# Loading half a weight matrix in three transfers instead of two, and splitting each transpose copy between VectorE and ScalarE

## Chip, cores and metric

The kernel runs on one core of one Trainium2 chip (trn2). The metric is the time of one launch on the device in microseconds; lower is better. Before the change the median of three runs is 178.41 us (177.83 to 178.98).

## What is computed

One input `x` (2048 tokens by 512, bf16) goes through two branches, and a gate per token mixes them. All matrices are bf16.

```python
# A: linear attention, 32 heads of 16
q, k, v = x @ wqkv                         # 512 -> 3 * 512
pq, pk = phi(q), phi(k)                    # phi(t) = where(t > 0, t + 1, exp(t)) + 1e-6
kv = einsum("bhsd,bhse->bhde", pk, v);  z = pk.sum(over tokens)
a = ((pq @ kv) / (pq . z + 1e-6)) @ wo
# B: gated feed-forward, F = 1376
b = (silu(x @ w1) * (x @ w3)) @ w2
g = sigmoid((x * gate_w).sum(-1))
out = g * a + (1 - g) * b
```

## The kernel before

Tokens are cut into 16 tiles of 128 (index `t`) and four blocks of 512. The model dimension of 512 is cut into four chunks of 128 (index `kc`), because a matmul contracts over the 128 partitions. A projection of one token tile is thus four matmuls, one for each `kc`, that accumulate in one bank of PSUM. Each of them has the transposed tokens `xT[:, kc, tile]` as its stationary operand (loaded by an LDWEIGHTS) and the weight rows `w[:, kc, :]` as its moving operand.

The order of TensorE (PE) is written out by hand (`manual_schedule` with `ENG.PE`); the other engines keep the order of the program in the stretch that matters here. The whole launch is one long run of matmuls:

1. **Head.** Lines 85 to 115 issue all loads. The SyncE (SP) queue gets `x` for the first two token tiles (L85, into `x_sb`), transposing DMAs that write the other token tiles straight into `xT` (L92, L95), more of `x` (L100) and then every weight but one. The ScalarE (ACT) queue gets only `wk`, the 512 key columns of `wqkv`, in two transfers: L86 brings `kc` 0 and 1, L87 brings `kc` 2 and 3. Behind them in ACT's own order stand a one-element exponential (L89), which makes ACT load its function table early, and ACT's later work.
2. **Warm-up.** PE runs nine matmuls on constants (`emit_warm`, L169) while the first loads are on their way.
3. **First transposes.** Token tiles 0 and 1 are not transposed by a DMA. `emit_xT(t)` (L177) transposes each in four 128x128 pieces on PE (L182). Two pieces (`kc` 0 and 1, then 2 and 3) share one PSUM tile `xTp` of 128x256; its tag `XP0` to `XP3` gives every pair a bank of its own. A pair then has to be copied from PSUM to `xT` in SBUF. The pair `h == 0` is copied by VectorE (DVE, L187), the pair `h == 1` by ACT (L189), 256 columns each.
4. **First key matmuls.** Lines 404 to 413 run `k` for token tiles 0 to 3. The order on PE starts with `(kc, t)` = (0,0), (1,0), (0,1), (1,1), (2,0), (3,0), and then the last two of tile 1, each through `emit_k_mm` (L191). `emit_k_phi` has ACT and DVE apply phi to the result.
5. **Keys and XP.** Lines 418 to 422 alternate four matmuls `XP += x^T pk` (`emit_xp`, L212) with four key matmuls of a later tile. `XP` for tile 2 onwards reads the `x_sb` rows that L100 loads.
6. **The rest**, which the change does not touch: query projections, kv and z, the feed-forward, normalisation and output, block by block, until the last token tile is stored.

Buffers: `wk_sb`, `x_sb` and `xT` are each allocated once, so no load waits for a buffer.

Of the kernel before, what the change touches and what calls it, by code (L numbers as in the profile page):

```python
# [8 lines left out]
ACT = mybir.ActivationFunctionType  # L9
# [8 lines left out]
def kernel(  # L18
# [12 lines left out]
    nc = tc.nc  # L31
    P = nc.NUM_PARTITIONS

    Bb, S, D = A_x.shape
# [31 lines left out]
    xT = consts.tile([P, KC, S], BF16, name="xT")  # L66
    wk_sb = consts.tile([P, KC, D], BF16, name="wk_sb")
# [9 lines left out]
    wqkv_r = A_wqkv.rearrange("(kc d) n -> d kc n", d=P)  # L77
# [5 lines left out]
    x_first = x2d[0 : TF * P, :].rearrange("(p j) d -> p j d", j=TF)  # L83
    out_first = out2d[0 : TF * P, :].rearrange("(p j) d -> j p d", j=TF)
    dq.dma_start(out=x_sb[:, 0:TF, :], in_=x_first)  # L85
    nc.scalar.dma_start(out=wk_sb[:, 0:2, :], in_=wqkv_r[:, 0:2, D : 2 * D])  # L86
    nc.scalar.dma_start(out=wk_sb[:, 2:4, :], in_=wqkv_r[:, 2:4, D : 2 * D])  # L87
    pre = consts.tile([1, 1], FP32, name="pre")
    nc.scalar.activation(out=pre[:], in_=nc.const_aps.tensor(0.0, [1, 1], FP32), func=ACT.Exp)  # L89
    for t in range(TF, TPB):  # L90
        tsl = slice(t * P, (t + 1) * P)
        dq.dma_start(out=xT[:, :, tsl], in_=x2d[tsl, :], transpose=True)  # L92
    x_cut = [TF, TPB + 2, 3 * TPB, NT]
    for tb in range(1, NTB):
        dq.dma_start(  # L95
            out=xT[:, :, tb * TB : (tb + 1) * TB], in_=x2d[tb * TB : (tb + 1) * TB, :],
# [7 lines left out]
    with nc.allow_non_contiguous_dma(reason="one gate weight per partition and chunk"):  # L104
        dq.dma_start(
            out=wr_sb[:, :, 2 * FR : NR], in_=gate_w.rearrange("(kc d o) -> d kc o", d=P, o=1)
# [3 lines left out]
    for fsl in (slice(0, FM // 2), slice(FM // 2, FM)):  # L110
# [12 lines left out]
        out=bm, in_=bm, pattern=[[-Dh, HPC], [0, Dh]], compare_op=ALU.is_ge, fill=0.0,  # L123
# [3 lines left out]
        out=bm, in_=bm, pattern=[[Dh, HPC], [0, Dh]], compare_op=ALU.is_ge, fill=0.0,  # L127
# [49 lines left out]
    def emit_xT(t):  # L177
        for h in range(2):
            xTp = psX.tile([P, 2, P], BF16, tag=f"XP{(2 * t + h) % 4}", name="xTp")
            for j in range(2):  # L180
                kc = 2 * h + j
                nc.tensor.transpose(  # L182
                    out=xTp[:, j, :], in_=x_sb[:, t, kc * P : (kc + 1) * P], identity=ident[:]
                )
            xT_t = xT[:, 2 * h : 2 * h + 2, t * P : (t + 1) * P]
            if h == 0:
                nc.vector.tensor_copy(out=xT_t, in_=xTp[:])  # L187
            else:
                nc.scalar.activation(out=xT_t, in_=xTp[:], func=ACT.Copy)  # L189

    def emit_k_mm(k_ps, t, kc):  # L191
        nc.tensor.matmul(  # L192
# [210 lines left out]

    k0 = [psM.tile([P, D], FP32, tag="mm", name=f"k0_{t}") for t in range(TPB)]
    emit_xT(0)
    emit_xT(1)
    for kc, t in ((0, 0), (1, 0), (0, 1), (1, 1), (2, 0), (3, 0)):
        emit_k_mm(k0[t], t, kc)
# [17 lines left out]
    with tc.manual_schedule(engines={ENG.DVE}):  # L426
# [18 lines left out]
        for dc in range(KC):  # L445
# [9 lines left out]
            out=z_sb[:].rearrange("p (b f) -> p b f", f=Q),  # L455
            in_=z_col[:, :, None].to_broadcast([P, NB, Q]),
# [3 lines left out]
        for c in range(KC):  # L460
# [10 lines left out]
            out=kvT_sb[:], in0=kvT_ps[:],  # L471
# [86 lines left out]
```

## Time and profile before

| what | value |
|---|---|
| median of three runs | 178.41 us (177.83 to 178.98) |
| span of the profiled execution, first to last instruction | 176.0 us |
| PE busy | 172.5 us, 98% of the span |
| DVE, ACT, POOL busy | 118.0, 64.8, 67.0 us |
| mean granted TensorE clock | 1.000 |
| bytes moved by DMA | 15.14 MB; HBM read 8.42 MB, written 2.10 MB |
| L86, L87 (`wk`), issue to landing | 3.4 and 3.7 us |
| L187, DVE copy of a transposed pair | 2 of 292 ns |
| L189, ACT copy of a transposed pair | 2 of 381 ns (mean) |

The profile is of one execution. Its span leaves out what lies before the first and behind the last recorded instruction; the median of the runs is 2.4 us longer than this span. Lines such as L187 are lines of the kernel as printed above. In a timeline row the first number is the start in us from the start of the span, the second is the duration (for several merged instructions, from the first's start to the last's end), and the brackets give the idle time of the engine ahead of it and what ended it. PE is the matmul itself, PEld the weight load ahead of it, SPq and ACTq are the sequencers that issue DMAs. Matmuls are pipelined, so a row of 16 of them is better read by its start-to-start distance than by the 379 ns that each is given.

### The profile page before, as it was taken

To read this page: it belongs to the slowest core of one execution; us is meant where nothing else is said; L and a number is where in the kernel's file an instruction comes from. 1 tells how busy PE (TensorE), PEld (TensorE's weight loads), DVE (VectorE), ACT (ScalarE), POOL (GpSimd) and SP (SyncE) were. 2 spreads that over 40 slices of the span, in tenths; PEclk is the share of its full clock that TensorE was granted. 3 is DMA by queue.
4 is the path that set the end of the run, shared out by engine and by line. 5 is a ranking of instruction groups with operands and counts; after the bars stand their busy time and mean duration, and the time that the engine had idled before them with its cause. 6 is when DMAs were issued, how large, how long until landed. Compare 5 with 4: busy or idle time off the path is not lost.

```text
span 176.0 us, 2619 instructions
## 1 busy us (share of the span) xinstructions
PE 172.5 (98%) x946; PEld 82.8 (47%) x946; DVE 118.0 (67%) x205; ACT 64.8 (37%) x122; POOL 67.0 (38%) x100
## 2 busy tenths in 40 slices
PE   7999999999999999999999999999999999999994
PEld 3444444464445454444454544444545444444463
DVE  0596858899999646697875466977754669776000
ACT  4524324466424333324343332333434323341222
POOL 7297655789019323282003232820032329100000
PEclk9999999999999999999999999999999999999999
DMA  5999999941002510126000201230002022300002
GB/s 180 204 226 295 271 296 378 351 138 26 8 0 60 71 48 27 41 62 87 0 0 7 65 14 56 56 76 2 0 11 67 7 67 56 64 0 4 30 30 60
DMA packets 29884, 15.14 MB, mean 86 GB/s; under 512 B 20944, under 2 KB 29232, under 8 KB 29872
## 3 DMA queue, kind: packets, MB, share of 16 engines
q1 hardware_dynamic: 29184, 14.41, 31.9%
q10 hardware_dynamic: 688, 0.57, 1.0%
q8 instruction: 7, 0.11, 0.3%
q14 instruction: 5, 0.04, 0.1%
HBM read 8.42 MB, written 2.10 MB: 60 GB/s over the span
## 4 chain that ended last, share of the span: by engine, by line
PE 98%; DVE 0%; issue 0%
PE o_ps L384 20%; PE up_ps L342 20%; PE gate_ps L334 19%; PE XP L212 8%; PE o_ps L375 8%; PE q_ps L225 8%; PE k_ps L192 6%; PE r_ps L249 3%; PE k L192 2%; PE o_ps L379 2%; PE warm L169 2%; PE gate L334 0%; PE kvT_ps L466 0%; PE W_ps L500 0%; DVE xT L187 0%; DVE o_last L393 0%
## 5 line engine op out<-in xcount | busy, mean ns | idle before, releaser
L342 PE MATMUL up_ps<-xT,w_sb 128*128 128x512 bf16 x160 | 41.1, 379 | 0.0
L334 PE MATMUL gate_ps<-xT,w_sb 128*128 128x512 bf16 x156 | 40.0, 379 | 0.0
L233 POOL TENSOR_TENSOR qz<-pq,z_sb 128x512 f32<-128x512 bf16 x16 | 18.5, 1163 | 54.0 <-DVE pq L153 54.0
L347 ACT ACTIVATE th<-gate_ps 128x512 bf16<-128x512 f32 x39 | 23.3, 597 | 39.3 <-PE gate_ps L334 38.9
L384 PE MATMUL o_ps<-w_sb,hT 128*128 128x512 bf16 (+3 forms) x180 | 37.5, 355 | 0.0
L349 DVE SCALAR_TENSOR_TENSOR gs<-th,gate_ps 128x512 bf16<-128x512 bf16 x39 | 26.6, 683 | 5.5 <-ACT th L347 5.1
L354 DVE TENSOR_TENSOR hT<-up_ps,gs 128x512 bf16<-128x512 f32 x40 | 27.5, 691 | 3.7 <-PE gate_ps L334 0.5
L150 DVE TENSOR_SCALAR phi_m<-phi_e 128x512 bf16<-128x512 bf16 x32 | 13.7, 429 | 20.9 <-ACT phi_e L148 20.8
L302 POOL TENSOR_TENSOR pqn<-pq,rden 128x256 bf16<-128x256 bf16 x32 | 19.0, 626 | 16.4 <-DVE rden L293 15.4
L384 PEld LDWEIGHTS <-hT 128*128 128x128 bf16 x180 | 16.9, 98 | 17.8
L342 PEld LDWEIGHTS <-w_sb 128*128 128x128 bf16 x160 | 15.7, 98 | 18.9
L334 PEld LDWEIGHTS <-w_sb 128*128 128x128 bf16 x159 | 15.4, 98 | 18.5 <-issue 0.2
L389 ACT ACTIVATE o_out<-o_ps,omg 128x512 bf16<-128x512 f32 x15 | 10.3, 687 | 28.8 <-PE o_ps L384 26.1
L202 POOL TENSOR_TENSOR pks<-pks,pk_sb 128x512 f32<-128x512 f32 x15 | 17.5, 1164 | 7.4 <-DVE pk_sb L153 6.7
L375 PE MATMUL o_ps<-W_sb,pqT 128*128 128x512 bf16 (+3 forms) x72 | 16.8, 355 | 0.0
L225 PE MATMUL q_ps<-wq_sb,xT 128*128 128x512 bf16 x64 | 16.4, 379 | 0.0
L212 PE MATMUL XP<-pk_sb,x_sb 128*128 128x512 bf16 x64 | 16.3, 379 | 0.0
L236 DVE TENSOR_REDUCE den<-qz 128x32 f32<-128x512 f32 x16 | 11.0, 685 | 7.9 <-POOL qz L233 7.8
L148 ACT ACTIVATE phi_e<-k_ps 128x512 bf16<-128x512 f32 x12 | 7.2, 597 | 14.5 <-PE k_ps L192 14.5
L148 ACT ACTIVATE phi_e<-q_ps 128x512 bf16<-128x512 f32 x16 | 9.6, 597 | 7.8 <-PE q_ps L225 7.8
L192 PE MATMUL k_ps<-wk_sb,xT 128*128 128x512 bf16 x48 | 12.3, 379 | 0.0
L153 DVE SCALAR_TENSOR_TENSOR pq<-q_ps,phi_m 128x512 bf16<-128x512 f32 x16 | 11.1, 691 | 0.5
(67 smaller groups left out, 119.4 us busy)
## 6 DMA issues: line engine op xcount, KB each, us to landing
w_sb<-in_B_w_dram SPq DMA_DIRECT2D x2, 1280.0 KB, 10.7
out_dram<-o_out SPq DMA_DIRECT2D x15, 128.0 KB, 1.7
w_sb<-in_B_w_dram SPq DMA_DIRECT2D x2, 640.0 KB, 9.9
x_sb<-in_A_x_dram SPq DMA_DIRECT2D x2, 512.0 KB, 5.1
x_sb<-in_A_x_dram SPq DMA_DIRECT2D x1, 768.0 KB, 5.1
wk_sb<-in_A_wqkv_dram ACTq DMA_DIRECT2D x2, 256.0 KB, 3.5
wq_sb<-in_A_wqkv_dram SPq DMA_DIRECT2D x1, 512.0 KB, 6.1
wv_sb<-in_A_wqkv_dram SPq DMA_DIRECT2D x1, 512.0 KB, 4.7
```

What stands on the lines that cost most here:

```text
L192: nc.tensor.matmul(k_ps[:], lhsT=xT[:, kc, t * P : (t + 1) * P], rhs=wk_sb[:, kc, :], start=(kc == 0), stop=(kc == KC - 1),)
L212: nc.tensor.matmul(XP_ps[dc][:], lhsT=x_sb[:, t, dc * P : (dc + 1) * P], rhs=pk_sb[:, t, :], start=(t == 0), stop=(t == NT - 1),)
L225: nc.tensor.matmul(q_ps[:], lhsT=xT[:, kc, ts_tok], rhs=wq_sb[:, kc, :], start=(kc == 0), stop=(kc == KC - 1),)
L233: nc.gpsimd.tensor_tensor(out=qz[:], in0=st[tb, "pq"][:, tt, :], in1=z_sb[:], op=ALU.mult)
L302: nc.gpsimd.tensor_tensor(out=pqn[:].rearrange("p (i c e) -> p c i e", i=NG, c=KC)[:, :, :, dsl], in0=st[tb, "pq"][:, tt, :].rearrange("p ...
L334: nc.tensor.matmul(gate_ps[:], lhsT=w1_sb[:, kc, fsl], rhs=xT[:, kc, tok_sl], start=(kc == 0), stop=(kc == KC - 1),)
L342: nc.tensor.matmul(up_ps[:], lhsT=w3_sb[:, kc, fsl], rhs=xT[:, kc, tok_sl], start=(kc == 0), stop=(kc == KC - 1),)
L347: nc.scalar.activation(out=th[:], in_=gate_ps[:], func=ACT.Tanh, scale=0.5)
L349: nc.vector.scalar_tensor_tensor(out=gs[:], in0=th[:], scalar=1.0, in1=gate_ps[:], op0=ALU.add, op1=ALU.mult)
L354: nc.vector.tensor_tensor(out=st[tb, "hT"][:, fc, :], in0=up_ps[:], in1=gs[:], op=ALU.mult)
L375: nc.tensor.matmul(o_ps[:], lhsT=st[tb, "pqT"][:, c, tsl], rhs=W_sb[:, c, a:b], start=(c == 0), stop=False,)
L384: nc.tensor.matmul(o_ps[:], lhsT=st[tb, "hT"][:, fc, tsl], rhs=w2_sb[:, fc, a:b], start=False, stop=(fc == FC - 1),)
```

## The change

`wk` now arrives in three transfers on ACT's queue: `kc` 0 alone, `kc` 1 alone, and `kc` 2 and 3 together. Each transposed pair is copied by two instructions of 128 columns, the even `kc` by DVE and the odd one by ACT, in place of one instruction of 256 columns on one of the engines. The order on PE, all other loads and all later work stay as they are.

```diff
-    nc.scalar.dma_start(out=wk_sb[:, 0:2, :], in_=wqkv_r[:, 0:2, D : 2 * D])
-    nc.scalar.dma_start(out=wk_sb[:, 2:4, :], in_=wqkv_r[:, 2:4, D : 2 * D])
+    for ksl in (slice(0, 1), slice(1, 2), slice(2, 4)):
+        nc.scalar.dma_start(out=wk_sb[:, ksl, :], in_=wqkv_r[:, ksl, D : 2 * D])
...
-            xT_t = xT[:, 2 * h : 2 * h + 2, t * P : (t + 1) * P]
-            if h == 0:
-                nc.vector.tensor_copy(out=xT_t, in_=xTp[:])
-            else:
-                nc.scalar.activation(out=xT_t, in_=xTp[:], func=ACT.Copy)
+            tsl = slice(t * P, (t + 1) * P)
+            nc.vector.tensor_copy(out=xT[:, 2 * h, tsl], in_=xTp[:, 0, :])
+            nc.scalar.activation(out=xT[:, 2 * h + 1, tsl], in_=xTp[:, 1, :], func=ACT.Copy)
```

## Prediction

> **What bounds the kernel now.** I read the page's chain of waits first, then the chain in order of time over the first 12 us, then the timeline of the stretch between the transposes and the first key matmul, and last what the DMA queues did there.
>
> ```profile
> PE 172.5 (98%) x946; PEld 82.8 (47%) x946; DVE 118.0 (67%) x205; ACT 64.8 (37%) x122; POOL 67.0 (38%) x100
> PE 98%; DVE 0%; issue 0%
> ```
>
> PE is busy all the time and is the chain. So the change can gain only where PE pauses, and lose only by adding a pause. Taken by start-to-start distance (0.216 us for 512 columns), the matmuls of the whole trace show few pauses: about 0.22 us between the last transpose and the first key matmul, 0.04 us at 11.30, and 0.19 us together near 41. The change touches the first.
>
> ```profile
> 3.84 0.13 PE xTp L182 x2
> 3.97 0.02 issue
> 3.99 0.30 DVE xT L187
> 4.29 0.05 issue
> 4.34 3.63 PE k L192 x16
> 7.97 0.86 PE XP L212 x4
> 8.83 0.86 PE k_ps L192 x4
> ```
>
> This is the chain in order of time (start, length, what). The only step of another engine on it is the first DVE copy, 0.30 us: the first key matmul waits for it. From 4.34 on PE runs without a hole.
>
> ```profile
> 3.62 0.49 PEld L182 LDWEIGHTS <-x_sb 128*128 128x128 bf16 x8
> 3.67 0.61 PE L182 MATMUL xTp<-ident,x_sb 128*128 128x128 bf16 x8
> 3.99 0.51 DVE L187 COPY xT<-xTp 128x256 bf16<-128x256 bf16 x2 [3.99 <-PE xTp L182]
> 4.10 0.66 ACT L189 ACTIVATE xT<-xTp 128x256 bf16<-128x256 bf16 x2 [0.79 <-PE xTp L182]
> 4.34 0.11 PEld L192 LDWEIGHTS <-xT 128*128 128x128 bf16 x2 [0.22 <-DVE xT L187]
> ...
> 11.30 0.11 PEld L212 LDWEIGHTS <-x_sb 128*128 128x128 bf16 x2 [0.37 <-DMA x_sb<-in_A_x_dram]
> ```
>
> These are timeline rows. Two things stand in them. The copies of different pairs overlap across the engines today (DVE from 3.99, ACT from 4.10), each released by PE. And at 11.30 PE's weight load waits for the `x_sb` transfer of L100, which landed at 11.26: a second fixed point, set by the DMAs and not by when the key matmuls began.
>
> ```profile
> q10 hardware_dynamic: 544, 0.52, 70.2%
> q1 hardware_dynamic: 446, 0.23, 35.7%
> ```
>
> These are the DMA queues between 2.5 and 4.7 us (packets, MB, share of 16 engines). q10 carries `wk`, q1 what SP issued. The engines are full there.
>
> **The copies.** Removed: 2 DVE copies of 292 ns and 2 ACT copies of 381 ns; added: 4 and 4 of 128 columns. The row of 128 columns does not exist, so I interpolate. DVE: the clamp L266 (128x2) takes 161 ns when nothing delays it, the 256-column copy 292, which is 0.52 ns a column and 226 ns at 128; ends 161 and 292. ACT: 331 ns at 192 columns (L255) and 597 at 512 (L148) give 0.83 a column, so 381 less 106 is 275; ends 203 (L269, 128x2) and 381. I take the middle values, since each lies on a line through rows of its own engine. Half the columns do not halve the time.
>
> The built order decides the rest: each of ACT's four copies now waits for DVE's semaphore, at the count of DVE's copy of the same pair, where before they waited for PE. The two halves of a pair do not run at once; ACT follows DVE. What is queued behind this wait on ACT is the next copy, then phi of `k` at 5.85.
>
> So: DVE's first copy still starts at 3.99 (both transposes of the pair are waited for) and ends at 3.99 + 0.23 = 4.22 in place of 4.29. With 0.05 us from DVE's end to PE's weight load, as in the rows above, matmul (0,0) starts at 4.27 rather than 4.34: 0.07 gained. Matmul (1,0) needed nothing further before and ran at 4.57. Now it needs ACT's copy: 4.22, plus 0.03 from DVE's end to ACT's start (as between L266 and L269: 37.90 to 37.93), plus 0.275, is 4.53, plus 0.05, is 4.58. So the second matmul is 0.01 us later than before, and the 0.07 is a short hole between the first and the second. Bounds: with the short ends, 3.99 + 0.16 + 0.03 + 0.20 + 0.05 = 4.43, and (1,0) follows (0,0), which starts at 4.21, after 0.23: 4.44, so 0.13 earlier. With the long ends, 3.99 + 0.29 + 0.03 + 0.38 + 0.05 = 4.74: 0.17 later.
>
> The next new wait is (1,1) on ACT's third copy. Today's two ACT copies start 0.28 apart at 0.38 each, so 0.10 overlaps; with 0.175 apart the third starts at 4.60, ends at 4.88 and releases PE at 4.93. The matmul is due at 4.58 + 2 x 0.216 = 5.01. It holds. With the long ends (third copy from 4.32 + 0.56 to 5.26, release 5.31) it would be 0.31 late, the upper bound of this part. The copies of `kc` 2 and 3 are due after 5.2, DVE's second ends by 4.4 and ACT's second by 4.71; ACT's last ends about 5.06, due at 5.88. No cost.
>
> The row for this is the overlap of 4.10 to 4.29 above: two engines read PSUM together there, from two different tiles. [...]
>
> [...]
>
> **The transfers.** Two more things stand in ACT's queue ahead of the table load: one more issue, and the last 256 KB later. The issues of 256 rows take 0.47 and 0.50 us, the 128 rows of L85 take 0.40. With 0.40 for the small ones the third issue starts at 0.80 + 2 x 0.43 = 1.67 in place of 1.30, ends at 2.16, and the table load (1.28) and the one-element exponential (0.20) end at about 3.7. ACT's first copy is due at 4.25: covered, with 0.5 to spare.
>
> `kc` 0 and 1 landed at 4.23 (issue 0.80 + 3.4); `kc` 0 alone cannot be later, and is due at 4.27. `kc` 2 and 3 landed at 4.96 (1.30 + 3.7) and are due at matmul (2,0), 5.22: 0.25 of slack. What hides the later issue is that the engines are busy with `kc` 0 and 1 until about 3.7: today's first packet of q10 is at 2.61, 1.34 after its issue ended, and by that the third transfer could start at 3.50, before the engines are free for it. So it costs nothing if that holds; if that cover is gone, the whole 0.37 shifts it to 5.33, 0.11 too late plus 0.04 for the release. SP's queue gets nothing, and no instruction of POOL's moves. The semaphores of SP's transfers shift by one place, onto transfers that landed long before.
>
> **What is late next.** Whatever is gained at 4.34 comes to rest at 11.30, where `x_sb` lands at 11.26 whenever the keys began; whatever is lost there is made up to 0.04. So the sum in the middle is 0.01 lost, less 0.04 of slack: zero. Against the span: 176.0; against the median of the runs: 178.4. Bounds of the copies: 0 (gain stopped at 11.30) to 0.31 - 0.04 = 0.27 later.
>
> **Rivals.** First, a true gain: the copies come out at the short ends and the `x_sb` landing moves up with them, 0.13 us, 178.3. For it speaks that DVE's copy is alone on the chain at 3.99; against it, the wait at 11.30 and the built order. 1 in 10.
>
> Second, slower: the third `wk` transfer comes late. From 4.21 on the transposing DMAs of q1 put packets on the same engines. If the third transfer's first packet comes 0.37 later than today's (about 4.07 instead of 3.70), it has to share them: alone its 0.26 MB take 0.76 us at the 345 GB/s of that window, shared equally up to 1.5, so its data end between 4.83 and 5.57, and with 0.44 from last packet (4.52) to landing (4.96) it lands between 5.27 and 6.01. Matmul (2,0) at 5.22 then stalls by 0.05 to 0.8 us. It decides from a landing at 5.18. It would read 178.5 to 179.2. Against it: the 0.2 us of cover above. 17 in 100.
>
> Third, `x` itself: L85 landed at 3.58 and PE's first transpose weight load followed at 3.62, with the last warm-up matmul at 3.57. A quicker start of `wk` packets beside `x` (first at 2.61, `x` done at 3.20) would move everything by as much, but 11.30 keeps its place: under 0.1 us. 3 in 100.
>
> **How the numbers follow.** The forecast, no change, has 68 in 100, 2 in 100 are for the unseen. About 1%, 1.8 us, is what a measurement can tell from no change; none of these cases reaches it. I leave 3 in 100 for faster and 5 for slower by that much, for what no row here shows. The scatter of the three runs, 0.6 to either side, is larger than every term: the low end is 177.83 less the gain of 0.13, 177.7; the high end is 178.98 plus 0.27, 179.25, which takes in the second rival's 179.2: 179.3.
>
> **What would show it.** Right: in the profile after, ACT's 128-column copies start at DVE's ends, not with them; the DVE row is near 226 and the ACT row near 275 ns; the second key matmul stands near 4.58, with a hole of some 0.1 before it; the weight load of `XP` still waits at about 11.30 for `x_sb`. Wrong: a wait of PE on a DMA between 5.2 and 6.0 (second rival), a start of the transposes away from 3.62 (third), or no wait at 11.30 and a shorter span (first). It would be wrong outright if the time moved by more than the scatter.

## The result

| | median of the runs | range |
|---|---|---|
| before, measured beside the change | 178.09 us | 177.83 to 178.98 |
| changed | 180.25 us | 179.52 to 180.81 |

The ratio is 1.0091, with a 95% interval of 1.0064 to 1.0117: about 1.6 us slower (0.0091 x 178.4). The two medians stand 2.2 us apart, slightly beyond the interval's upper end of 2.1 us; what follows goes by the ratio. Runs more than 1.5% above the fastest of their kernel, two of e14's twelve further down, do not enter the ratios. The prediction, 178.4 with a range to 179.3, was wrong.

**The profile after.** Busy time and chain of waits of the page of the changed kernel:

```profile
span 178.6 us, 2624 instructions
PE 172.9 (97%) x946; PEld 82.8 (46%) x946; DVE 118.3 (66%) x207; ACT 65.0 (36%) x124; POOL 67.1 (38%) x100
PE 94%; DMA 3%; ACTq 0%; DVE 0%; issue 0%
```

No engine does noticeably more work than before (PE 172.5, ACT 64.8), and yet the span is 2.6 us longer. The new entry is "DMA 3%": a transfer now stands on the chain. In the chain in order of time, from 3 us on (start, length, what), it has a name:

```profile
1.74 5.17 DMA wk_sb<-in_A_wqkv_dram
6.91 0.04 issue
6.95 2.75 PE k L190 x12
9.70 0.86 PE XP L210 x4
```

The third `wk` transfer (`kc` 2 and 3, L87 after the change) is issued at 1.74 and lands at 6.91, 5.17 us later. Before, the same 256 KB were issued at 1.30 and landed at 4.96. The timeline of the changed kernel between 3.9 and 7 us (lines behind the copies have moved up by two: L186 is DVE's copy, L187 ACT's, L190 the key matmul):

```profile
3.92 0.45 PEld L182 LDWEIGHTS <-x_sb 128*128 128x128 bf16 x8 [0.30 <-DMA x_sb<-in_A_x_dram]
...
4.24 0.62 DVE L186 COPY xT<-xTp 128x128 bf16<-128x128 bf16 x4 [4.24 <-PE xTp L182]
4.50 0.79 ACT L187 ACTIVATE xT<-xTp 128x128 bf16<-128x128 bf16 x4 [0.78 <-DVE xT L186]
...
4.53 1.15 PE L190 MATMUL k<-wk_sb,xT 128*128 128x512 bf16 x4
4.83 0.14 PEld L190 LDWEIGHTS <-xT 128*128 128x128 bf16 x2 [0.21 <-ACT xT L187]
```

Read from the top: the first transpose starts at 3.92, not 3.67, because `x` landed at 3.88. ACT's copies are released by DVE's. The first four key matmuls run from 4.53, with the short hole ahead of the weight load at 4.83. Then PE has nothing until the row of the chain at 6.95.

From the first `XP` matmul to the last matmul PE takes 165.4 us in both traces, so whatever is lost at the head arrives at the end. The start-to-start distances of the matmuls add up as follows:

| step on PE | before | after | change |
|---|---|---|---|
| first transpose starts | 3.68 | 3.92 | +0.25 |
| from there to the first key matmul | 0.67 | 0.60 | -0.06 |
| first to second key matmul | 0.23 | 0.35 | +0.12 |
| fourth to fifth (`kc` 2, waits for `wk`) | 0.22 | 1.65 | +1.44 |
| wait for `x_sb` at 11.30 | 0.05 | none | -0.05 |
| sum | | | +1.70 |
| start of the last matmul | 173.22 | 174.90 | +1.68 |

That leaves some 0.9 us of the 2.6. SP's waits, by releaser (total us, times, longest), first for the kernel before, then for the changed one:

```profile
SPq L553 <- DMA out_dram<-o_last: 0.8, 2, 0.7
```

```profile
SPq L551 <- DMA out_dram<-o_last: 1.7, 1, 1.7
```

This is the wait for the last store, behind all the work. In the changed kernel 15 of the 16 parts of that store landed by 1.97 us after the last matmul's start, as before, and one at 2.74. The DMA queues between 176.4 and 177.8 us show what was there:

```profile
q1 hardware_dynamic: 62, 0.01, 3.4%
q14 instruction: 1, 0.01, 1.6%
```

One 8 KB packet of an instruction queue started 1.60 us after the last matmul's start, beside the store's last packets; in the profile before, the corresponding one comes at 3.40, when everything has landed. The prediction says nothing of the end of the kernel.

One more thing belongs to reading the span. In the 17 profiles of the changed kernel and of the experiments, whose own device time is known, that time is 1.67 to 1.75 us above the span. So the execution profiled before took about 176.0 + 1.7 = 177.7, as fast as the fastest of its runs, and comparing the two spans makes the change look worse (2.6 us) than the ratio of the runs does (1.6).

### The profile page after: what moved, and what is told of

Read it like the earlier page. It is cut to its first block, busy times and chain, and to the rows that moved or that the text cites. A ratio compares the mean times of both kernels' runs of the same rounds, so it can differ in the third digit from the quotient of the medians.

```text
span 178.6 us, 2624 instructions
## 1 busy us (share of the span) xinstructions
PE 172.9 (97%) x946; PEld 82.8 (46%) x946; DVE 118.3 (66%) x207; ACT 65.0 (36%) x124; POOL 67.1 (38%) x100
## 4 chain that ended last, share of the span: by engine, by line
PE 94%; DMA 3%; ACTq 0%; DVE 0%; issue 0%
PE o_ps L382 19%; PE up_ps L340 19%; PE gate_ps L332 19%; PE o_ps L373 8%; PE q_ps L223 8%; PE XP L210 8%; PE k_ps L190 6%; PE r_ps L247 3%; DMA wk_sb<-in_A_wqkv_dram 3%; PE o_ps L377 2%; PE k L190 2%; ACTq L87 0%; PE gate L332 0%; PE kvT_ps L464 0%; PE W_ps L498 0%; DVE o_last L391 0%
## 5 line engine op out<-in xcount | busy, mean ns | idle before, releaser
L387 ACT ACTIVATE o_out<-o_ps,omg 128x512 bf16<-128x512 f32 x15 | 10.3, 687 | 28.7 <-PE o_ps L382 28.7
L190 PE MATMUL k_ps<-wk_sb,xT 128*128 128x512 bf16 x48 | 12.3, 379 | 0.0
```

The costliest lines, as they stand in the source:

```text
L190: nc.tensor.matmul(k_ps[:], lhsT=xT[:, kc, t * P : (t + 1) * P], rhs=wk_sb[:, kc, :], start=(kc == 0), stop=(kc == KC - 1),)
```

## The experiments

My theory was that the late third transfer carries the loss and the copies nothing. The rival was the copies, and, inside the theory, several reasons why the transfer is late. "Landed" is the landing of `kc` 2 and 3, "first XP" the start of the first `XP` matmul, which carries every delay of the head. "Store" is the landing of the last part of the last store after the start of the last matmul.

| kernel | ratio to before (95%) | issued, landed | first XP | store |
|---|---|---|---|---|
| before | 1 | 1.30, 4.96 | 7.81 | 1.97 |
| changed | 1.0091 (1.0064 to 1.0117) | 1.74, 6.91 | 9.54 | 2.74 |
| e1 copies only | 0.9988 (0.9965 to 1.0012) | 1.29, 5.13 | 8.24 | 1.97 |
| e2 three loads only | 1.0065 (1.0037 to 1.0092) | 1.73, 7.19 | 9.82 | 1.98 |
| e8 changed again | 1.0091 (1.0062 to 1.0120) | 1.74, 6.89 | 9.52 | 2.71 |
| e3 third load on SP | 1.0015 (0.9989 to 1.0041) | 1.26, 5.11 | 8.49 | 1.96 |
| e4 4 KB between two loads | 1.0054 (1.0025 to 1.0082) | 1.82, 6.39 | 9.02 | 1.97 |
| e12 second load late | 1.0039 (1.0015 to 1.0063) | 1.72, 6.40 | 9.14 | 1.97 |
| e7 second half cut | 1.0033 (1.0007 to 1.0058) | 1.82, 5.88 | 8.38 | 1.97 |
| e5 4 KB first on SP | 1.0088 (1.0054 to 1.0122) | 1.73, 5.85 | 8.98 | 2.86 |
| e9 plain load first | 180.48 us, one execution | 1.74, 7.08 | 9.71 | 2.76 |
| e10 transposing DMAs held | 184.09 us, one execution | 1.74, 5.47 | 11.11 | 2.99 |
| e6 own banks, two loads | 1.0015 (0.9989 to 1.0040) | 1.30, 5.09 | 8.74 | 1.97 |
| e13 changed, one ACT instruction less | 1.0078 (1.0051 to 1.0104) | 1.74, 6.71 | 9.33 | 1.97 |
| e15 e5, one ACT instruction less | 1.0051 (1.0033 to 1.0069) | 1.73, 6.00 | 8.62 | 1.98 |
| e14 before, three ACT instructions more | 1.0038 (1.0013 to 1.0063) | 1.29, 5.19 | 9.18 | 2.76 |
| e17 the same again | 1.0015 (0.9989 to 1.0041) | 1.30, 5.16 | 8.07 | 1.97 |
| e16 before, two more | 0.9997 (0.9973 to 1.0021) | 1.30, 5.12 | 8.14 | 1.97 |

The first `XP` matmul of a single profile must not be read as the kernel's: before, e1, e16 and e17 differ by 0.4 us with the same loads, and e6 and e14 stand later still without any wait for `wk`, for a reason given in the last section. The profiled execution of e14 is the slowest of its runs, so of its times only the place of its packets at the end is read.

Single profiles differ in a second place. In e7, e10, e12, e14 and e15 PE waits another 0.8 to 1.1 us near 58 us (61 in e10) for a transposing DMA of a later stage (`pqT`), in the other profiles it does not. e14 has the loads of the kernel before, so this wait doesn't need a late `wk`; how often each kernel has it is not known, and ratios that differ by a few thousandths may carry it. The lowest time of each kernel is blurred less. It is 177.7 to 177.9 us in all kernels that load `wk` as before, 178.4 in e3, 178.5 in e7 and e15, 178.8 and 178.9 in e12 and e4, 179.0 in e2, and 179.3 to 179.5 in e13, e5, e8 and the changed kernel.

**Which half of the change loses?** e1 takes the loads back, e2 the copies, and e8 is the changed kernel once more.

```diff
 e1, against the changed kernel
-    for ksl in (slice(0, 1), slice(1, 2), slice(2, 4)):
-        nc.scalar.dma_start(out=wk_sb[:, ksl, :], in_=wqkv_r[:, ksl, D : 2 * D])
+    nc.scalar.dma_start(out=wk_sb[:, 0:2, :], in_=wqkv_r[:, 0:2, D : 2 * D])
+    nc.scalar.dma_start(out=wk_sb[:, 2:4, :], in_=wqkv_r[:, 2:4, D : 2 * D])
 e2, against the kernel before
-    nc.scalar.dma_start(out=wk_sb[:, 0:2, :], in_=wqkv_r[:, 0:2, D : 2 * D])
-    nc.scalar.dma_start(out=wk_sb[:, 2:4, :], in_=wqkv_r[:, 2:4, D : 2 * D])
+    for ksl in (slice(0, 1), slice(1, 2), slice(2, 4)):
+        nc.scalar.dma_start(out=wk_sb[:, ksl, :], in_=wqkv_r[:, ksl, D : 2 * D])
```

> Two wk transfers as before, only the copies split. My theory (the loss of the change is the late landing of kc 2 and 3, the copies are worth nothing): kc 2 and 3 land near 4.96, no wait of PE on wk, the second key matmul near 4.58 with a hole of about 0.1 us before it, the time within 0.3 us of before (ratio 0.998 to 1.002). Rival (ACT's copies behind DVE's carry the loss): 1 to 2 us slower than before.

> Three wk transfers, the copies whole as before. My theory: the whole loss of the change, about 1.6 us (ratio 1.007 to 1.012): x lands near 3.9 instead of 3.58, kc 2 and 3 near 6.9 instead of 4.96, and PE waits 1.2 to 1.5 us for them. Rival (it is the copies): within 0.3 us of before.

> The changed kernel once more, beside the others on the same chip. My theory: kc 2 and 3 land between 6.4 and 7.3, PE waits 1.2 to 1.6 us for them, ratio 1.006 to 1.012; the last store's 0.9 us longer landing of the first profile does not return (1.5 us or less from the last issue on ACT to the last landing).

The copies alone make no difference (0.9988), the loads alone 1.0065, that is 1.2 us. The chain of e2 carries the same piece as the changed kernel's:

```profile
1.73 5.46 DMA wk_sb<-in_A_wqkv_dram
7.19 0.04 issue
7.23 2.75 PE k L192 x12
```

So the loads carry the loss of the head. In e8 the third transfer landed at 6.89 again. PE's pause for it was only some 0.96 us by the start-to-start distance, below what I expected, because the first of the four matmuls ahead of it ran at the slower pace in that execution (the 512-column warm-up matmuls of the kernel before stand 427 ns apart, its key matmuls 216; the four key matmuls took 1.54 us here and 1.15 in the changed kernel); the end of the wait (6.93) is fixed by the landing and not by its length. The long wait for the last store, which I expected not to return, did return (2.71). The gap between 1.0065 and 1.0091 was open until the last group of runs; the two intervals overlap.

**Is it the place in the queue?** e3 issues the third transfer from SP, between `x` and the first transposing DMA, at 1.26. The other three leave the copies as before and make the issue late in other ways. e4 puts a 4 KB transfer into a scratch tile between the two old loads. e12 has the two old loads, and the second waits for a memset by GpSimd on its destination (ACT's order is written by hand around them, so that nothing overtakes it). e7 cuts the second half rather than the first.

```diff
 e3, against the changed kernel
+    dq.dma_start(out=wk_sb[:, 2:4, :], in_=wqkv_r[:, 2:4, D : 2 * D])
-    for ksl in (slice(0, 1), slice(1, 2), slice(2, 4)):
+    for ksl in (slice(0, 1), slice(1, 2)):
 e4, against the kernel before
     nc.scalar.dma_start(out=wk_sb[:, 0:2, :], in_=wqkv_r[:, 0:2, D : 2 * D])
+    nc.scalar.dma_start(out=scr[:], in_=x2d[0:P, 0:16])
     nc.scalar.dma_start(out=wk_sb[:, 2:4, :], in_=wqkv_r[:, 2:4, D : 2 * D])
 e12, against the kernel before
     nc.scalar.dma_start(out=wk_sb[:, 0:2, :], in_=wqkv_r[:, 0:2, D : 2 * D])
+    nc.gpsimd.memset(wk_sb[:, 2:4, 0:384], 0.0)
     nc.scalar.dma_start(out=wk_sb[:, 2:4, :], in_=wqkv_r[:, 2:4, D : 2 * D])
 e7, against the kernel before: one loop in place of the two loads
+    for ksl in (slice(0, 2), slice(2, 3), slice(3, 4)):
+        nc.scalar.dma_start(out=wk_sb[:, ksl, :], in_=wqkv_r[:, ksl, D : 2 * D])
```

> The changed kernel, but kc 2 and 3 are issued from SP, between x and the first transposing DMA. Theory A (the third transfer is late because it shares the DMA engines with the transposing DMAs that got in front of it): kc 2 and 3 land by 5.3, PE waits less than 0.2 us for them; the transposed tiles 2 and 3 land about 0.5 later than before and PE may wait 0.2 to 0.5 us for those; the time 0 to 0.6 us above before. Theory B (three small transfers are slow by themselves, whatever runs beside them): kc 2 and 3 still land after 6, about 1.5 us slower.

> The kernel before with its two wk transfers of 256 KB, and a transfer of 4 KB (128 rows of 32 bytes into a scratch tile) issued on ACT between them, so that the second one is issued about 0.43 us later, as in the change, while the first half stays whole. Theory A (what counts is that the last transfer is issued later and meets the transposing DMAs): it lands between 6 and 7, PE waits 0.8 to 1.5 us, 1.0 to 1.6 us slower than before. Theory B (what counts is that the first half is cut in two): it lands by 5.4, under 0.3 us slower.

> The kernel before with its two wk transfers of 256 KB and nothing between them, but the second waits for a POOL memset and is issued near 1.75 instead of 1.30. Theory A (the later issue lets the transposing DMAs get in front; neither the cut nor a third transfer is needed): kc 2 and 3 land between 6 and 7, 0.6 to 1.3 us slower than before. Rival (a third transfer in ACT's queue is needed): they land by 5.4 and the time is within 0.4 us of before.

> The kernel before, its copies whole; wk in three transfers again, but the first half whole and the second cut: kc 0 and 1, kc 2, kc 3. Theory A: kc 0 and 1 and kc 2 land by 4.7, x lands as before; only the third transfer (128 KB, issued near 1.8) meets the transposing DMAs and lands between 5.5 and 6.4, where the matmul of kc 3 is due near 5.43 at full clock: PE waits 0.1 to 0.9 us, 0.2 to 0.9 us slower than before. Rival (three transfers are slow whatever their order): as the change, 1.2 us slower or more.

e3 keeps three loads and the new copies and loses nothing that the ratio could tell (1.0015, an interval that includes 1), though its lowest time stays 0.7 us above the lowest before. Its chain has no `wk` in it, only `x` and PE:

```profile
0.81 3.10 DMA x_sb<-in_A_x_dram
3.90 0.05 issue
3.95 1.03 PE xTp L183 x8
4.98 3.67 PE k L191 x16
```

e12 has neither a cut nor an additional transfer, only a second load issued 0.42 us later, and it lands 1.44 us later (6.40) and costs 0.70 us (1.0039). e4 agrees (6.39, 0.96 us, just under the 1.0 expected). In these two profiles PE's pause for the load is at most 0.35 us, less than the 0.8 expected of e4, because the key matmuls ahead of it ran at the slower pace (0.43 us apart in e12, from 5.09 to 5.94); so their costs rest on the ratios and the lowest times, and e12's may hold some of the wait near 58 us. e7 cuts the load at another place, so only 128 KB are late; they land at 5.88, and the ratio is 0.59 us above before. In its profile PE does not wait for them, so where these 0.59 us lie is not shown. The three landings came out as the theory had it: the later issue made the load late, without a cut (6.39, 6.40) and with one (5.88). That the cut itself costs a little more (e2's 7.19 against e12's 6.40) is not told apart by these intervals.

**What delays it on the way?** The queues between 4.2 and 5.6 us (busy tenths of the DMA engines in 40 slices; packets, MB and share of 16 engines by queue). In the kernel before:

```profile
DMA  9899999999999999999999999999999997889989
q1 hardware_dynamic: 1298, 0.32, 103.5%
q10 hardware_dynamic: 77, 0.06, 13.2%
```

In the changed kernel:

```profile
DMA  3835929599949959729098995997967995949799
q10 hardware_dynamic: 168, 0.17, 80.2%
q1 hardware_dynamic: 261, 0.06, 23.1%
```

Before, `wk` (q10) is nearly through and the transposing DMAs (q1, 256-byte packets of 18 ns) fill the engines afterwards. In the changed kernel both run mixed and move 0.23 MB instead of 0.38. The 168 packets of `wk` took 0.802 x 16 x 1.4 us / 168 = 107 ns on average, where one of these 1 KB packets took 46 ns from 3 to 4 us of the kernel before, where q10 runs beside plain loads only. The mixing starts early: from 3 to 4 us before has 347 `wk` packets and not one of the transposing DMAs; the changed kernel has 182, and 268 of 256 bytes.

The third transfer itself began nearly on time: the 257th `wk` packet, which is about its first, starts at 3.95 (3.65 in e8, 3.68 before). But the first transposing packet came at 3.55 and thus ahead of it, where before it came at 4.21, behind it. This order divides the profiles. In the six in which transposing packets came first (changed, e2, e4, e8, e12, e13) the last 256 `wk` packets took 83 to 105 ns on average; in those in which `wk` came first they took 46 to 57 ns, also beside transposing packets (e3, whose third load runs on SP's queue, is not counted).

Three experiments moved the other traffic. e9 puts the plain 512 KB load of L100's first part ahead of all transposing DMAs. e10 holds the transposing DMAs and all behind them on SP until `kc` 2 and 3 have landed (by a 4 KB transfer that reads `wk_sb`). e5 puts a 4 KB transfer of scratch ahead of the transposing DMAs, so that they are issued 0.45 us later. All three are the changed kernel otherwise.

```diff
 e9
+    dq.dma_start(out=x_sb[:, x_cut[0] : x_cut[1], :], in_=x_r[:, x_cut[0] : x_cut[1], :])
     for t in range(TF, TPB):
...
-        dq.dma_start(out=x_sb[:, x_ts, :], in_=x_r[:, x_ts, :])
+        if tb > 1:
+            dq.dma_start(out=x_sb[:, x_ts, :], in_=x_r[:, x_ts, :])
 e10, all of SP's order by hand
+    with tc.manual_schedule(engines={ENG.SP}):
+        dq.dma_start(out=scr[:], in_=wk_sb[:, 2, 0:16])
+        for t in range(TF, TPB):
...
 e5
     dq.dma_start(out=x_sb[:, 0:TF, :], in_=x_first)
+    dq.dma_start(out=scr[:], in_=x2d[0:P, 0:16])
```

> The changed kernel, but SP issues a plain load (512 KB of x_sb, the first transfer of L100) between x and the first transposing DMA, so that the third wk transfer has plain traffic beside it. What counts is its landing and its packets, not the time, since the transposed tiles come later. Theory A (it is late because it runs among the transposing DMAs): its 1 KB packets take 46 to 60 ns, as they do alone, and it lands between 5.0 and 5.8 although it shares the engines with 512 KB. Theory B (any traffic put in front of a late third transfer delays it as much): it lands at 6.2 or later.

> The changed kernel, but SP issues its transposing DMAs only when kc 2 and 3 have landed (a 4 KB copy out of that half stands in front of them on SP). Again the landing counts; the time is some 2 to 4 us longer since all later loads are held. Theory A: with x and wk alone on the engines the third transfer lands by 5.1 although it is issued at 1.74 and wk comes in three transfers. Theory C (three transfers, or the late issue, are slow by themselves): it lands at 5.8 or later.

> The changed kernel with its three wk transfers on ACT, and a transfer of 4 KB into a scratch tile issued on SP between x and the first transposing DMA, so that this DMA is issued near 1.70 instead of 1.26 and the third wk transfer stands to it as the second one did in the kernel before. Theory A (the order against the first transposing DMA decides): kc 2 and 3 land by 5.3, PE waits less than 0.2 us for them, and the time is 0 to 0.7 us above before, some of it for transposed tiles that land later. Rival (three transfers on ACT's queue, or the late issue of the third by itself, decide): kc 2 and 3 land after 6 as in the change, 1.2 to 2 us slower than before.

e9 is a miss for the narrower theory, that only transposing traffic delays `wk`. Its queues between 4.2 and 5.6 us:

```profile
DMA  9999999999999999999999999999999899989969
q1 hardware_dynamic: 300, 0.29, 59.0%
q10 hardware_dynamic: 238, 0.23, 49.0%
```

The `wk` packets are short again (0.490 x 22.4 us / 238 = 46 ns) and the engines are full, but the third transfer lands at 7.08 all the same, since it shares the engines with a plain load. It began at 5.07 only, and 175 of its 256 packets started before the first transposing packet (5.70). So plain traffic that got in front of it made it late as well; the longer packets (83 to 105 ns) go with transposing packets that came first.

e10 gives the other bound. With no transposing DMA issued, the transfer lands at 5.47, between the 5.1 and the 5.8 that the theories expected, and 12 of its 16 parts by 5.05. Of the 1.95 us between 4.96 and 6.91, about 0.5 would by this one execution be its own later issue and the cut, and 1.4 other traffic. (The 184 us are the price of the held transposing DMAs and say nothing more.)

e5 landed at 5.85, a whole us earlier than the changed kernel but not by 5.3 as expected, and its time did not improve: 1.0088 (four runs). In its profile PE does not wait for `wk` at all, since the key matmuls ran at the slower pace (the sixteen took 4.05 us, before 3.63). `x` landed at 4.01 and tile 3's transposed tokens at 7.37, so I first took the loss as moved to these. The next group changed that reading.

**Copies in their own banks.** e6 keeps the two old loads and gives the two halves of tile 0's first pair a PSUM bank each (one pair of tile 1 goes to a bank of the key matmuls); only this first pair is split between the engines.

```diff
+        own = [psX.tile([P, 1, P], BF16, tag=f"XP{j}", name="xTp") for j in range(2)]
+        for j in range(2):
+            emit_piece(own[j], 0, 0, j)
+        nc.vector.tensor_copy(out=xT[:, 0, 0:P], in_=own[0][:, 0, :])
+        nc.scalar.activation(out=xT[:, 1, 0:P], in_=own[1][:, 0, :], func=ACT.Copy)
+        rest = ((psX, "XP2", 0, 1), (psX, "XP3", 1, 0), (psM, "mm", 1, 1))
```

> The kernel before with two wk transfers; of the first pair of token tile 0 each half has a PSUM bank of its own, and DVE copies one and ACT the other; the other three pairs are copied whole as before (one lies in a bank of the key matmuls' pool). If the shared bank is what puts ACT behind DVE, ACT's copy now starts within 0.06 us of DVE's, and the second key matmul follows the first without a hole (0.22 to 0.23 us after it, at full clock); the key matmuls begin 0.07 us earlier than before against the transposes. The time within 0.3 us of before (ratio 0.997 to 1.002). If ACT's copy still starts after DVE's end, it was not the bank.

The timeline of e6:

```profile
4.06 0.23 DVE L186 COPY xT<-xTp 128x128 bf16<-128x128 bf16 x1 [4.06 <-PE xTp L178]
4.17 0.28 ACT L187 ACTIVATE xT<-xTp 128x128 bf16<-128x128 bf16 x1 [0.85 <-PE xTp L178]
```

Now ACT is released by PE, not by DVE, and starts 0.12 us before DVE's copy ends (4.29). The 0.11 between the two starts (0.06 expected) is the distance of the two transposes at the slower pace (the eight took 1.03 us here, 0.61 before). The second key matmul follows the first by 0.43 us, which is the distance at that pace, so without a hole; the 0.07 us of an earlier start can't be told at it. So the row "ACT behind DVE" of the changed kernel came from what its two halves share. e6 gives each half a tile and a bank of its own; which of the two it is, this run does not tell apart. In time it brings nothing that could be measured (1.0015).

**The end of the kernel.** e5 and the gap between e2 and the changed kernel led back to the final wait. The trace records 195 instructions of ACT in the changed kernel (192 before, 193 in e2, 194 in e1). The last 8 KB instruction packet starts 3.3 to 3.4 us after the last matmul's start in every profile with 192 or 193, and about 1.8 in e1 and e3 with 194; it started at 1.57 to 1.61 in the five with 195. Only in these five did a part of the last store land late. The trace shows it packet by packet: in the five, the last eight 128-byte packets of the store's queue start when the instruction packet ends (at 1.96, after 1.60 + 0.36, in the changed kernel; at 2.46, after 1.58 + 0.88, in e10); in all others the last one starts by 1.61. e13 and e15 take one ACT instruction from the changed kernel and from e5; e14 and e17 add three one-element copies, which nobody reads, to the kernel before, and e16 two.

```diff
 e13, e15
+            if t == 1 and h == 1:
+                nc.vector.tensor_copy(out=xT[:, 3, tsl], in_=xTp[:, 1, :])
+            else:
                 nc.scalar.activation(out=xT[:, 2 * h + 1, tsl], in_=xTp[:, 1, :], func=ACT.Copy)
 e14, e17 (e16: range(2)), behind the loop over the first key tiles
         emit_k_phi(k0[t], t)
+    for _ in range(3):
+        nc.scalar.activation(out=pre[:], in_=pk_sb[0:1, 0, 0:1], func=ACT.Copy)
```

> The change as it stands, but the last of ACT's four copies (tile 1, kc 3) is made by DVE, so ACT has 194 recorded instructions instead of 195. The final wait of SP for the last store (SPq at the end, DMA out_dram<-o_last) was 0.7 to 1.0 us in the profiles whose ACT has 192 to 194 records, and 1.7 to 2.0 us in the five that have 195; there one 8 KB packet of the queue that fetches instructions starts 1.58 to 1.61 us after the last matmul's start, ahead of the last part of the last store. Theory F (the length of ACT's program decides when that packet comes): the packet starts near 1.84 after the last matmul's start, as in the copies-only kernel, the final wait is 0.7 to 1.0 us, and the ratio is 1.003 to 1.0075, like that of the three loads alone (1.0065), 0.4 to 0.9 us under the changed kernel. Rival L (the long final wait comes with the late head, or by chance): the wait stays 1.6 to 2.0 and the ratio 1.0075 to 1.011. The wait of PE for the third wk transfer (landing 6.8 to 7.3) stays by both.

> The kernel before with three ACT instructions of one element (a copy of one number that nobody reads) between the exponentials of key tiles 2 and 3, so that ACT has 195 recorded instructions and not 192; loads and copies as before. The three lie in ACT's idle time (about 1 us of the 1.72 us that a key tile takes). Theory F: an 8 KB packet of the instruction queue starts 1.55 to 1.65 us after the last matmul's start, one part of the last store lands 0.7 to 1.0 us late, the final wait of SP is 1.5 to 2.0 us, and the ratio is 1.003 to 1.006 with no wait of PE for wk. Rival L: final wait 0.7 to 1.0, ratio 0.998 to 1.002.

> The earlier kernel with a 4 KB transfer ahead of the transposing DMAs on SP's queue (it moves a scratch tile that nobody reads; 1.0088 with 195 ACT records and a final wait of 1.9), now with the last of ACT's four copies made by DVE. Theory F with the late landing as the rest: third wk transfer again at 5.6 to 6.1, final wait 0.7 to 1.0 us, ratio 1.002 to 1.0055, so that most of the loss it seemed to keep at the head was at the end. Rival L, or a loss moved into later transposed tiles: ratio 1.007 to 1.011.

> The kernel before with two of the one-element ACT instructions instead of three, so 194 recorded ACT instructions: the control for the kernel with three. Theory F: the last 8 KB packet of the instruction queue starts near 1.84 after the last matmul's start, no part of the last store waits (all 16 landed by 2.0 after that start), the ratio is 0.998 to 1.002 and the time 0.3 to 0.9 us under that of the kernel with three. Rival: the added instructions themselves cost something at the head; then two cost about as much as three, and the ratio is 1.002 to 1.005.

> The kernel before with three of them once more, beside the one with two on the same chip. Theory F: packet at 1.55 to 1.65 after the last matmul's start, one part of the last store 0.7 to 1.0 us late, ratio 1.002 to 1.005. Rival (the added instructions): ratio 1.002 to 1.005 too, but no more than 0.1 us over the kernel with two.

SP's wait for the last store in e13:

```profile
SPq L554 <- DMA out_dram<-o_last: 1.0, 1, 1.0
```

One ACT instruction less, and the packet starts at 1.81 and all parts of the store land by 1.97, with the third `wk` transfer nearly as late as ever (6.71). The same in e15 and e16 (1.84, 1.83). In e14, with the loads and copies of before, the packet starts at 1.62 and one part lands at 2.76. So the late store is not a consequence of the late head. But the count does not settle it alone: e17 is the same kernel as e14, and in its profiled execution the packet came at 1.81 and nothing was late, against what I expected. With 195 the packet came in front in six profiles of seven.

The times do not fix the price. e14 is 0.68 us over the kernel before (0.2 to 1.1), e17, the same kernel, 0.27 with an interval that includes zero, e16 -0.05; e15 is 0.66 under e5, with intervals that overlap. e13 is only 0.23 under the changed kernel, and its 1.0078 lies just above the theory's range and inside the rival's: by its time it tells nothing apart. Half a us is an estimate from these. e15, with the store in time, is 0.9 us over the kernel before (1.0051), close to e4 and e12 with their similar landing. So a good part of the loss that e5 seemed to keep may lie at the other end.

## Why the prediction was wrong, point by point

- **Copies: right.** DVE's row has 225 and 215 ns for 226 predicted, ACT's 271 to 296 for 275. ACT starts 0.03 us after DVE's end (4.47, 4.50). From the first transpose to the first key matmul 0.06 us is gained (0.07 predicted), and a hole of 0.12 follows (0.1). e1 has no measurable effect. ACT waited for DVE where the two halves share a bank and a tile; in e6, where each has its own, it started at 4.17, ahead of DVE's end at 4.29.
- **Transfers, "it costs nothing if that holds": the step that failed.** The issue times were nearly right (1.67 to 2.16 predicted, 1.74 to 2.19 measured), and so was ACT, which was ready in time. The failing sentence is the cover: "the engines are busy with `kc` 0 and 1 until about 3.7". I read the full engines as a wall behind which a later issue loses nothing. The start was covered, as said (about 3.95, and 3.65 in e8, for 3.68 before). But the engines are shared: in the changed kernel the transposing packets, issued at 1.26 in both, came in from 3.55 on rather than from 4.21, ahead of the third transfer, whose packets then took 99 ns on average in place of 46. It landed at 6.91 instead of 4.96, and PE waited 1.44 us. e12 and e4 show that the later issue without a cut costs 0.7 to 1.0 us by the ratios, e3 that a load issued early costs nothing that the ratio could tell.
- **The price "if that cover is gone", 0.11 + 0.04, was too small by a factor of ten.** It shifted the transfer by the delay of its issue. The wait measured 1.44 us in this execution; in e8, at the slower pace, 0.96.
- **Second rival: the right mechanism, undersized, and given 17 in 100.** It had the transposing packets come from 4.21 on, shared the bandwidth of a full window equally, and so came to data that end by 5.57 and a landing by 6.01. The transposing packets came from 3.55 on, and the mixed stretch moves 0.23 MB where the full one moves 0.38, so half of a full window was not an upper bound: the last `wk` packet ended at 5.99. From there to the landing it was 0.92 us instead of the 0.44 taken over from before, so the landing was 6.91.
- **Third rival, `x` late: present, and larger than the "under 0.1 us" that it was given (0.25 us here).** In the nine profiles with a first `wk` transfer of 128 KB `x` landed at 3.72 to 4.11, in the nine without at 3.58 to 3.78: later in most, by 0.1 to 0.3 us. Some of the nine have an additional transfer on SP too; the changed kernel, e2, e8 and e13, which have none, span the same range.
- **"Whatever is gained at 4.34 comes to rest at 11.30": wrong as a fixed point.** The landing of those `x_sb` rows was 11.26 in the profile before, and between 10.3 and 11.0 in the other profiles with the same loads (e1, e6, e14, e16, e17). The wait for it was an accident of the profiled execution.
- **Missing altogether: the end.** I counted the instructions that the change adds to ACT for ACT's time only. With them an 8 KB instruction packet also came in front of the end of the last store, as in six of the seven profiles in which ACT has 195: 0.77 us in the trace, and by the times about half a us, an estimate.
- **The sum against the median.** I took 2.4 us between span and median; it is 1.7 for one execution, and the other 0.7 was this execution's luck.

What stays open: why a 0.4 us later issue lets transposing DMAs, issued at the same time in both kernels, come first (3.55 for 4.21; what sets that order is not in the trace), and the exact size of the two terms. The head's 1.2 us is the ratio of e2, and in a single execution it depends on when the matmuls reach their full pace; the store's half a us is not clear of zero in most pairs of runs.

## What to carry to other kernels

Before cutting a load into more transfers, ask which traffic of other queues takes the place that each later piece gives up: here the full DMA window was shared and was no cover, and the piece came out later by several times the delay of its issue (1.95 us for 0.44). What cured it here was to issue the piece that is due next ahead of the competing traffic, on that traffic's own queue (e3, landing at 5.11), and even that only brought the old time back. Look at the last store and at the instruction packets beside it in both profiles, since here one stood in front of it in six of the seven profiles with three ACT instructions more, and in none of the others.

## What was unexpected in the hardware

- **A plain load beside transposing DMAs.** Its 1 KB packets took 46 ns beside a plain load (e9) and 107 ns on average among transposing packets in the changed kernel, and there the engines together moved 164 GB/s instead of the 270 of the kernel before (all between 4.2 and 5.6 us). The profiles divide by which came first: `wk` packets took 46 to 57 ns where they were ahead, and 83 to 105 where the transposing ones were.
- **Instruction packets compete with data.** These traces show packets of 16,384 bytes on one instruction queue and 8,192 on the other. Those of 8,192 bytes took 0.3 to 0.9 us, and eight small store packets behind one waited for its end (1.60 + 0.36 = 1.96 in the changed kernel), so that the last part of the store landed at 2.74 instead of 1.97.
- **The matmuls reach their full pace at different times.** The distance of 512-column matmuls goes from 427 to 216 ns by 3.7 us in the profile before and by 3.9 in the one after (told from the 128-column matmuls there, 107 and then 56 ns apart), but at about 4.9 in e1, 6.0 in e6 and 6.9 in e14, with the same warm-up, while the granted clock reads 0.996 to 1.000 for every span, and 1.00 from 0.8 to 3.6 us of the kernel before, where the distance is 427 ns. What sets the moment, no run here shows. It moves the head by about 1 us and more (first `XP` 7.81 before, 8.74 in e6, 9.18 in e14, none with a wait for `wk`), which I estimate to be a good part of the scatter of the kernel before (177.67 to 180.03 over 35 runs), and it can hide part of a wait in a single profile, as in e8.
